# Layer B keys: softmax weights multiplied into the features instead of the values, token sums of 128 feature rows by 68 columns

## The chip, the cores and the metric

The kernel runs on one core of a Trainium2 chip. A core has five engines that run side by side and meet only at semaphores: TensorE (PE, the matrix unit, which writes to PSUM), VectorE (DVE), ScalarE (ACT), GpSimd (POOL) and SyncE (SP, which here issues the DMA transfers). The metric is the device time of one execution in microseconds (us); the figure for the kernel before is the median of three runs.

## What is computed

Two pairs of layers are applied to a token matrix of 2048 rows by 512 columns, A, B, A, B, each with a layer norm ahead of it and its result added to the rows. Layer A is attention inside four segments of 512 tokens plus a memory carried between segments. Layer B, which the change touches, is linear attention with softmax features, for 32 heads of 16 columns:

```
pq = einsum('bhsd,hdf->bhsf', q, w_phi)
pk = einsum('bhsd,hdf->bhsf', k, w_phi)
phi_q = concatenate([softmax(pq), softmax(-pq)], axis=-1)
phi_k = concatenate([softmax(pk), softmax(-pk)], axis=-1)
kv = einsum('bhsf,bhsd->bhfd', phi_k, v)
z = einsum('bhsf->bhf', phi_k)
o = einsum('bhqf,bhfd->bhqd', phi_q, kv) / (einsum('bhqf,bhf->bhq', phi_q, z)[..., None] + 1e-06)
```

A key thus has two softmaxes of 16 features for each head, one of each sign, and each has its own sum of exponentials. One divided by that sum is the key's softmax weight. The token sum kv needs feature times weight times value, and it does not matter to the sum which of the two factors carries the weight.

## The kernel before

A `Graph` collects operations with what each reads and writes, and tiles from fixed pools of buffers. Nothing is scheduled when the kernel is built: a compressed table, `ORDER`, holds for all operations their order, then one byte for each that names its engine, then one byte for each tile that names its buffer. `emit` walks that order, gives each engine its instructions in it, and adds the semaphore waits. An operation whose result may be made by ACT or DVE (`evac`, which copies PSUM to SBUF) has its engine from that table. So the order of every engine is fixed beforehand, and each engine works strictly through its own list.

PSUM is used as four buffers of 128x1024 (`D` in the profile). SBUF pools that matter here: `p2` (128x1024 bf16, in the profile `p`, like `p1`), `pT` (value tiles) and `pS` (small sums).

The stages in time are: layer A's four segments of the first pair, with layer B's keys of each segment (`b_keys`) as soon as its rows are done; then the four `b_query` of that pair, which need the token sums of all segments, mixed with layer A of the second pair and with its keys; last the four `b_query` of the second pair. All token sums of a pair must be complete before its first query is divided, so the keys of segments 2 and 3 (c = 2 and 3) stand just before that point.

`b_keys` takes the tokens in units of two tiles of 128 tokens (n = 2) or one (n = 1): per pair of layers seven units of two and two units of one, the latter in segment 3. For a unit of two it does this:

1. `BK` projects the keys with the folded weight, 16 matmuls of 512 columns on 64 rows (line 341, a helper that also records all other projections).
2. `kexp` on ACT (line 351, the helper of every ACT function): two exponentials of 128x1024, one of each sign, into two tiles.
3. `Zred` on DVE (line 1003): two sums over 16 features, giving 32 sums for each token and sign.
4. The weights, one over the sums: on DVE (`rZ`, line 393) for c = 0 and 1, on ACT as Ln and Exp (`zkl`, line 351) for c = 2 and 3. They are written into row 16 of the value tile `Vt` (pool `pT`).
5. `BV` projects the values; then `Vt` multiplies the values by the weights, once for each sign. For c = 0 to 2 one DVE operation for each token tile reads PSUM and writes 1024 columns (line 1039). For c = 3 the values are first copied to SBUF (`BVe`) and two DVE operations of 512 columns follow for each tile (line 1031).

When four tiles are through (three and one in segment 3), `KV` adds up the tokens: for each of eight slots (a group of eight heads and a sign) the 128 exponentials of the eight heads are the matmul's weights, and 136 columns of `Vt` (17 by 8 heads) move through. Each token tile takes 16 matmuls, two for each slot, because the 128 tokens are split into two halves of 64 rows that run side by side in the array. Over the two pairs these are 512 matmuls `D<-pT,p` of line 341, in two PSUM buffers for each of the ten parts. `kv_add` adds each PSUM buffer into `KV32` on DVE (line 969), and at the last part multiplies by a 0/1 mask, because only the blocks of equal heads are wanted: `Rkv` (line 973) and the column of sums `Rz1` (line 976). `Zq` in `b_query` (line 326) uses `Rz1`, `N` uses `Rkv`.

`setup` makes the constants and `fold_weights` the folded weights. There the value weight is permuted by four `evac` named `perm`, and `Wbd`, from which the folded weights come, is made from `w_phi` and the mask.

## Time and profile before

| | |
|---|---|
| median of three runs | 459.82 us (459.4 to 461.3) |
| the profiled execution | 464.63 us |
| its span in the profile | 462.9 us |
| POOL busy | 59.2 us (13% of the span) |
| the DMA engines' mean share, queue q1 | 41.3% |
| granted TensorE clock, mean | 0.998 |

The profile is of one execution. It gives each engine's busy time, groups of equal instructions (line of the kernel, engine, operation, what is written and read, how often; then total busy time, mean duration of one in ns, and the idle time before them), the instructions in order of time, and the chain of work that ended last, followed back from the last instruction. An instruction's duration holds a fixed part that overlaps with the next one, so the distance between two starts is what one costs in a row of equal ones. A name with `<-` reads "written from".

### The profile page before, as it was taken

The numbers are of one execution on the slowest core, as the hardware profiler recorded it, in microseconds if no ns is written. First come the engines' busy times: TensorE is split into PE (matmuls) and PEld (weight loads), VectorE is DVE, ScalarE is ACT, GpSimd is POOL, SyncE is SP. The second block draws the span as 40 slices with busy tenths as digits, with TensorE's granted clock in tenths as the row PEclk, the third lists the DMA queues.
The fourth block names the chain that finished last, engine by engine and source line by source line (L and its number), as shares of the span: only waits on it lengthen the run. The fifth ranks groups of instructions, "written<-read, shape, count | busy, mean of one in ns | idle before, by whom it ended". The sixth has DMA issues, their size and how long they took to land.

```text
span 462.9 us, 26150 instructions
## 1 busy us (share of the span) xinstructions
PE 431.9 (93%) x12085; PEld 293.1 (63%) x12085; DVE 409.3 (88%) x760; ACT 418.2 (90%) x559; POOL 59.2 (13%) x143
## 2 busy tenths in 40 slices
PE   8999879899999989998899998999999989899896
PEld 4666647567666666765455767666676567556553
DVE  6999978798799987887999999998898896899897
ACT  6999989899999998689999999999999899577992
POOL 2530023001101001100330212110011020110000
PEclk9999999999999999999999999999999999999999
DMA  8967664354334231100356575365332423400156
GB/s 260 207 135 126 107 112 83 59 120 65 66 73 98 28 50 27 36 3 6 45 106 111 81 98 97 73 110 78 46 50 37 111 49 42 47 13 3 38 83 195
DMA packets 105168, 36.71 MB, mean 79 GB/s; under 512 B 91731, under 2 KB 105059, under 8 KB 105059
## 3 DMA queue, kind: packets, MB, share of 16 engines
q1 hardware_dynamic: 104226, 34.50, 41.3%
q8 instruction: 95, 1.56, 1.4%
q10 hardware_dynamic: 800, 0.52, 0.4%
q14 instruction: 15, 0.11, 0.1%
q0 software_dynamic: 32, 0.02, 0.0%
HBM read 10.76 MB, written 6.55 MB: 37 GB/s over the span
## 4 chain that ended last, share of the span: by engine, by line
PE 58%; ACT 20%; DVE 12%; DMA 4%; issue 3%; POOL 1%; SPq 0%; DVEq 0%; ACTq 0%
PE D L341 38%; PE D L326 20%; ACT p L351 12%; ACT pP L351 6%; DVE stats L594 3%; DMA pX<-p 2%; DVE X L956 2%; DMA p<-p 2%; DVE p L615 1%; DVE pQ L681 1%; DVE p L1120 1%; ACT pS L351 1%; POOL rstd L604 1%; DMA X<-in_A_x_dram 1%; DVE p L360 1%
## 5 line engine op out<-in xcount | busy, mean ns | idle before, releaser
L351 ACT ACTIVATE p<-D 128x1024 bf16<-128x1024 f32 (+1 forms) x228 | 223.6, 1027 | 14.9 <-PE D L341 12.1
L351 ACT ACTIVATE pP<-D 128x640 bf16<-128x640 f32 (+2 forms) x192 | 149.7, 830 | 8.8 <-PE D L326 7.8
L326 PE MATMUL D<-pK,pQ 64*128 64x256 bf16 (+6 forms) x1792 | 111.4, 227 | 4.5 <-ACT pP L351 1.6
L326 PEld LDWEIGHTS D<-pK,pQ 64*128 64x128 bf16 x1792 | 65.3, 93 | 37.6 <-ACT pP L351 6.9
L326 PE MATMUL D<-pW,pP 64*128 64x50 bf16 (+1 forms) x3072 | 85.0, 181 | 0.8 <-ACT pP L351 0.4
L326 PEld LDWEIGHTS D<-pW,pP 64*128 64x128 bf16 x3072 | 68.8, 93 | 6.5 <-issue 1.3
L602 POOL TENSOR_SCALAR rstd<-mv 128x1 f32<-128x1 f32 x60 | 16.9, 285 | 347.2 <-DVE mv L595 346.9
L326 PE MATMUL D<-pW,p 64*128 64x50 bf16 (+1 forms) x2048 | 49.4, 181 | 0.9 <-issue 0.8
L326 PEld LDWEIGHTS D<-pW,p 64*128 64x128 bf16 x2048 | 43.6, 93 | 4.5 <-issue 1.2
L956 DVE TENSOR_TENSOR X<-X,D 128x1024 bf16<-128x1024 bf16 (+1 forms) x36 | 39.2, 1097 | 5.6 <-PE D L341 5.0
L594 DVE BATCH_NORM_STATS2 stats<-X 128x6 f32<-128x512 bf16 x63 | 42.1, 681 | 1.7 <-DMA X<-in_A_x_dram 1.6
L1003 DVE TENSOR_REDUCE pS<-p 128x64 f32<-128x1024 bf16 (+1 forms) x36 | 39.1, 1091 | 2.1 <-ACT p L351 1.9
L326 PE MATMUL D<-tri,rep 64*128 64x64 bf16 (+1 forms) x384 | 39.9, 197 | 0.5 <-issue 0.5
L341 PE MATMUL D<-pX,WA_q 64*128 64x512 bf16 (+1 forms) x288 | 37.1, 353 | 1.3 <-ACT p L351 1.3
L341 PE MATMUL D<-pX,WA_k 64*128 64x512 bf16 (+1 forms) x288 | 37.0, 353 | 0.2 <-ACT pP L351 0.2
L341 PE MATMUL D<-WB_k,pX 64*128 64x512 bf16 (+1 forms) x288 | 33.5, 353 | 3.9 <-DMA pX<-p 3.1
L604 POOL TENSOR_TENSOR rstd<-rstd,mhalf 128x1 f32<-128x1 f32 x60 | 35.9, 603 | 4.0
L341 PE MATMUL D<-WB_v,pX 64*128 64x512 bf16 (+1 forms) x288 | 34.4, 353 | 1.8 <-issue 1.8
L341 PE MATMUL D<-WA_o,p 64*128 64x512 bf16 (+1 forms) x288 | 33.1, 352 | 1.6 <-DMA p<-p 1.5
L341 PE MATMUL D<-WB_o,p 64*128 64x512 bf16 (+1 forms) x288 | 32.6, 353 | 1.8 <-ACT pP L351 0.8
L341 PE MATMUL D<-WA_v,pX 64*128 64x512 bf16 x256 | 33.0, 377 | 0.8 <-DVE p L360 0.8
L341 PE MATMUL D<-pX,WB_q 64*128 64x512 bf16 x256 | 32.8, 376 | 0.2
(123 smaller groups left out, 675.7 us busy)
## 6 DMA issues: line engine op xcount, KB each, us to landing
v_rows<-pV SPq DMA_DIRECT2D x16, 272.0 KB, 3.1
pW<-v_rows SPq DMA_DIRECT2D x64, 68.0 KB, 3.1
out_dram<-X SPq DMA_DIRECT2D x7, 256.0 KB, 2.7
X<-in_A_x_dram SPq DMA_DIRECT2D x3, 512.0 KB, 5.8
pX<-in_B_wqkv_dram SPq DMA_DIRECT2D x3, 512.0 KB, 5.0
p<-p SPq DMA_TRANSPOSE x73, 3.1
pX<-p SPq DMA_TRANSPOSE x54, 3.5
WA_k<-in_A_wk_dram SPq DMA_DIRECT2D x2, 256.0 KB, 5.3
```

The source lines that it names most:

```text
L326: ins = e.matmul(out_ap, lhsT, rhs, start=st, stop=sp, tile_position=(basep(lhsT), basep(out_ap)))
L341: ins = e.matmul(out_ap, lhsT[64 * hf:64 * hf + 64], rhs[64 * hf:64 * hf + 64], start=k == 0 and i == 0, stop=k == 1 and i == len(lists[hf ...
L351: return self.g.op({"act": (dur, lambda e: e.activation(out_ap(), in_ap(), func, scale=scale))}, reads, writes, opens, label=label)
L360: "dve": ((340 if fast else n / 0.96 + 65), lambda e: e.tensor_copy(out_ap(), in_ap()))}
L594: v(lambda e: e.bn_stats(self.stats[:, t, :], self.X[:, t, :]), 602, [R("X", t)], [R("st", t)], label="bn")
L602: v(lambda e: e.tensor_scalar(rs, self.mv[:, t, 1:2], LN_EPS, None, op0=ALU.add), 170, [R("mv", t)], [R("rstd", t)], eng="pool", label="rstd")
L604: v(lambda e: e.tensor_tensor(rs, rs, self.mhalf[:], ALU.pow), 540, [R("rstd", t), R("mhalf")], [R("rstd", t)], eng="pool", label="rstd")
L615: v(lambda e: e.tensor_scalar(xn.t[:], self.X[:, t, :], self.mv[:, t, 0:1], self.rstd[:, t:t + 1], op0=ALU.subtract, op1=ALU.mult), 300, [ ...
L681: ch = {"dve": (129 + n / 3.84, lambda e, sl=sl, out=out: e.tensor_scalar(out(), src(), self.m4[:, sl:sl + 1], None, op0=ALU.mult))}
L956: self.v(lambda e: e.tensor_tensor(X(), X(), src(), ALU.add), 65 + 512 * n / 0.96, pr + xr, xr, label="res")
L1003: fn = lambda e, sgn=sgn, eo=eo, Z=Z, n=n: e.tensor_reduce(Z.t[:, 0:64 * n].rearrange("p (k s h) -> p k s h", k=n, s=2)[:, :, sgn, :], eo( ...
L1120: v(lambda e, Ns=Ns, Tm=Tm, w=w, shape=shape: e.tensor_tensor(shape(Tm.t[:]), shape(Ns.t[:]), w(), ALU.mult), 600, [Ns, AB[0]], [Tm], labe ...
```

## The change

The weight goes into the exponentials. The value tile becomes a plain copy of the projected values, with a 17th row that is set to 1 once for each buffer in `setup`. The columns of the folded weights and of the value weight are permuted so that heads lie in fours; an exponential tile now belongs to one token tile and holds, for each group of four heads, both signs side by side (128 columns).

For a unit of two, `kexp` is four ACT operations of 512 columns instead of two of 1024. `Zred` is again two of 1024 columns, but the 16 features that it sums now lie four elements apart. The weights are written to a small tile; for c = 2 and 3 ACT makes them with one Ln and one Exp of 128 (before, one Ln of 128 and two Exp of 64). The new `kn` multiplies the exponentials in place on DVE, one operation of 1024 columns for each token tile. `BVe` copies the values out of PSUM in all units. `KV` has eight slots again, each a group of four heads with both signs, and 68 moving columns (17 by 4 heads), so that one PSUM buffer holds what two held. `kv_add` therefore runs once for each part, and the masked copies at its end are made in four pieces of 64 rows each, `Rkv` and `Rkz`, in which a piece may move from one half of the partitions to the other.

Pool `p2` grows from 19 to 21 buffers, `pT` shrinks from 5 to 4, and `ORDER` is a new table. What the engine bytes of the two tables say:

| operations | before | after |
|---|---|---|
| all on PE, ACT, DVE | 1185, 558, 760 | 1165, 583, 766 |
| `kexp` on ACT | 36 | 64 |
| `zkl` on ACT | 18 | 12 |
| `BVe` on ACT | 6 (2 of 1024 columns, 4 of 512) | 11 (7 and 4) |
| `BVe` on DVE | 0 | 7 (of 1024) |
| `Vt`, then `kn`, on DVE | 40 | 36 |
| `KVacc` on DVE, ACT | 19, 1 | 10, 0 |
| `Rkv` and `Rkz` on DVE | 8 | 16 |
| `perm` on ACT, DVE | 2, 2 | 0, 4 |
| `Vev` (layer A's values) on ACT, DVE | 5, 11 | 3, 13 |

Six more copies and a mask go from one of the two engines to the other: to ACT one `Kev`, one `Km`, one `ote` and two `xnTe`; to DVE one `folde` and one `Macc`. In the new order the four `kexp` of a unit alternate between the two token tiles, except for seven pairs of neighbours that read the same half of a PSUM buffer. At the end of segment 3 the order on DVE is the last `KVacc`, four `Rkz`, four `Rkv`.

```diff
-        self.KV32 = sb("KV32", [128, 8, 136], F32)
-        self.Rkv = sb("Rkv", [128, 8, 16, 8], BF16)
+        self.KV32 = sb("KV32", [128, 8, 68], F32)
+        self.Rkv = sb("Rkv", [128, 8, 16, 4], BF16)
+        self.h4 = sb("h4", [128, 4], F32)
...
-        self.pT = pool("pT", N_VT, [128, 2, NG, 17, 8], BF16, {}, ("Vt",))
+        self.pT = pool("pT", N_VT, [128, 2, 8, 17, 4], BF16, {}, ("Vt",))
...
-        v(lambda e: e.tensor_copy(self.Rz1[:, :, 1, :], self.H8[:, None, :].to_broadcast([128, 8, 8])), 130,
-          [R("H8")], [R("RzH")])
+        v(lambda e: e.tensor_reduce(self.h4[:], self.ident[:].rearrange("p (a h) -> p h a", h=4), AX.X, ALU.add), 250, [R("ident")], [R("h4")], label="one")
+        v(lambda e: e.tensor_copy(self.Rz1[:].rearrange("p i k (u h) -> p (i k u) h", h=4), self.h4[:, None, :].to_broadcast([128, 32, 4])), 210,
+          [R("h4")], [R("RzH")] + [R("Rz", q, h) for q in range(2) for h in range(2)], label="one")
+        for i, tp in enumerate(self.pT.tensors):
+            self.pT.init[i] = two(lambda e, tp=tp: e.memset(tp[:, :, :, 16, :], 1.0), 200.0, 130.0)
...
+            self.evac(lambda g=g: self.WB["v"][:, g, :].rearrange("p (a d h) -> p a d h", a=8, h=4),
+                      lambda g=g: self.WBraw["v"].t[:, g, :].rearrange("p (a h d) -> p a d h", a=8, h=4),
                       512, [self.WBraw["v"]], [R("WBv", g)], label="perm")
...
+        for u in range(2):
+            v(lambda e, u=u: e.tensor_tensor(Wbd.t[:].rearrange("p (g u j h) -> p u g h j", g=NG, u=2, h=4)[:, u],
+                                             self.wphi_st[:, :, None, :].to_broadcast([128, NG, 4, 16]),
+                                             self.H8[:, None, 4 * u:4 * u + 4, None].to_broadcast([128, NG, 4, 16]), ALU.mult), 340,
+              [R("wphi"), R("H8")], [Wbd[u]])
...
-    def kv_add(self, ps, q, first, last):
+    def kv_add(self, ps, first, last):
...
+        src = lambda: ps.t[:].rearrange("p (b x) -> p b x", b=2)[:, :, 0:272]
+        dst = lambda: self.KV32[:].rearrange("p (b k) c -> p b (k c)", b=2)
         if first:
-            self.evac(dst, src, 136 * n, [ps[0]], [R("KV32", q)], label="KVacc")
+            self.evac(dst, src, 544, [ps[0]], [R("KV32")], label="KVacc")
...
+            v(lambda e: e.tensor_tensor(dst(), dst(), src(), ALU.add), 65 + 544 / 0.96, [ps[0], R("KV32")], [R("KV32")], label="KVacc")
         if last:
...
+            for sgn in range(2):
+                for hf in range(2):
+                    ri, ro = slice(64 * sgn, 64 * sgn + 64), slice(64 * hf, 64 * hf + 64)
+                    kv = lambda ri=ri, hf=hf: self.KV32[ri].rearrange("p (g u) (c h) -> p g u c h", u=2, h=4)[:, :, hf]
+                    v(lambda e, kv=kv, ri=ri, ro=ro, sgn=sgn: e.tensor_tensor(self.Rkv[ro].rearrange("p (g s) c h -> p g s c h", s=2)[:, :, sgn], kv()[:, :, 0:16, :],
+                                                                              self.h4[ri, None, None, :].to_broadcast([64, NG, 16, 4]), ALU.mult),
+                      65 + 256 / 0.96, [R("KV32"), R("h4")], [R("Rkv", sgn, hf)], label="Rkv")
+                    v(lambda e, kv=kv, ri=ri, ro=ro, sgn=sgn, hf=hf: e.tensor_tensor(self.Rz1[ro].rearrange("p (g s) k h -> p g s k h", s=2)[:, :, sgn, 0, 4 * hf:4 * hf + 4],
+                                                                                     kv()[:, :, 16, :], self.h4[ri, None, :].to_broadcast([64, NG, 4]), ALU.mult),
+                      85, [R("KV32"), R("h4")], [R("Rz", sgn, hf)], label="Rkz")
...
     def b_keys(self, L, c, parts):
...
                 S = self.T(self.pD, "gen")
                 Z = self.T(self.pS, "Z")
                 Et = [self.T(self.p2, "ET") for _ in range(n)]
...
+                cols = lambda E: E.t[:].rearrange("p (g s f h) -> p g s f h", g=8, s=2, h=4)
+                zs = lambda k, Z=Z: Z.t[:, 64 * k:64 * k + 64].rearrange("p (g s h) -> p g s h", g=8, s=2)
+                ws = lambda k, Z=Z: Z.t[:].bitcast(BF16)[:, 256 + 64 * k:256 + 64 * k + 64].rearrange("p (g s h) -> p g s h", g=8, s=2)
                 for k, tt in enumerate(u):
+                    E = Es[tt] = Et[k]
+                    for sgn in range(2):
+                        self.act(lambda E=E, sgn=sgn: E.t[:].rearrange("p (a g s x) -> p a g s x", a=2, g=4, s=2)[:, :, :, sgn, :],
+                                 lambda S=S, u=u, k=k: self.tview(S, u, k).rearrange("p (a g x) -> p a g x" if len(u) == 2 else "p a (g x) -> p a g x", **({"a": 2} if len(u) == 2 else {}), g=4),
+                                 ACT.Exp, 512, [S[512 * k]], [E[sgn]], scale=1.0 - 2.0 * sgn, label="kexp")
+                        if n == 1:
+                            v(lambda e, E=E, sgn=sgn, k=k, zs=zs, cols=cols: e.tensor_reduce(zs(k)[:, :, sgn, :], cols(E)[:, :, sgn].rearrange("p g f h -> p g h f"), AX.X, ALU.add),
+                              65 + 512 / 0.96, [E[sgn]], [Z[(k, sgn)]], label="Zred")
+                    if n == 2:
+                        v(lambda e, E=E, k=k, Z=Z: e.tensor_reduce(Z.t[:, 64 * k:64 * k + 64], E.t[:].rearrange("p (a f h) -> p a h f", a=16, h=4), AX.X, ALU.add),
+                          65 + 1024 / 0.96, [E[0], E[1]], [Z[(k, 0)], Z[(k, 1)]], label="Zred")
+                allz = [Z[(k, sgn)] for k in range(n) for sgn in range(2)]
+                allw = [Z[("w", k, sgn)] for k in range(n) for sgn in range(2)]
+                if n == 2 and (L, c) not in ZKD:
+                    self.act(lambda Z=Z: Z.t[:, 0:128], lambda Z=Z: Z.t[:, 0:128], ACT.Ln, 128, allz, allz, psum=False, label="zkl")
+                    self.act(lambda Z=Z: Z.t[:].bitcast(BF16)[:, 256:384], lambda Z=Z: Z.t[:, 0:128], ACT.Exp, 128, allz, allw, scale=-1.0, psum=False, label="zkl")
+                for k, tt in enumerate(u):
+                    E = Es[tt]
+                    for sg in ((0,), (1,)) if n == 1 else ((0, 1),):
+                        a, b = sg[0], sg[-1] + 1
+                        if not (n == 2 and (L, c) not in ZKD):
+                            v(lambda e, k=k, a=a, b=b, zs=zs, ws=ws: self.recip(e, ws(k)[:, :, a:b, :], zs(k)[:, :, a:b, :]), self.dur_recip(32 * (b - a)),
+                              [Z[(k, x)] for x in sg], [Z[("w", k, x)] for x in sg], label="rZ")
+                        v(lambda e, E=E, k=k, a=a, b=b, cols=cols, ws=ws: e.tensor_tensor(
+                            cols(E)[:, :, a:b], cols(E)[:, :, a:b], ws(k)[:, :, a:b, None, :].to_broadcast([128, 8, b - a, 16, 4]), ALU.mult) if b - a == 1 else e.tensor_tensor(
+                            cols(E).rearrange("p g s f h -> p (g s) f h"), cols(E).rearrange("p g s f h -> p (g s) f h"),
+                            ws(k).rearrange("p g s h -> p (g s) h")[:, :, None, :].to_broadcast([128, 16, 16, 4]), ALU.mult),
+                          65 + 535 * (b - a) / 2, [Z[("w", k, x)] for x in sg] + [E[x] for x in sg], [E[x] for x in sg], label="kn", port=True)
                 ps = self.T(self.pD, "gen")
...
+                Vt = self.T(self.pT, "Vt")
+                for k, tt in enumerate(u):
+                    Vts[tt] = (Vt, k)
+                self.tproj(ps, lambda dt: self.WB["v"][:, dt, :], [R("WBv", g) for g in range(NG)], u, lhs, [xT[tt] for tt in u], opens=[Vt], label="BV")
+                self.evac(lambda Vt=Vt, n=n: Vt.t[:, 0:n].rearrange("p k (b g) c h -> p (k b) g (c h)", b=3 - n)[:, :, :, 0:64],
+                          lambda ps=ps, n=n: ps.t[:].rearrange("p (a x) -> p a x", a=2)[:, :, 0:256 * n].rearrange("p a (g x) -> p a g x", x=64), 512 * n, [ps[0], ps[512]][:n], [Vt], label="BVe")
+            ps = self.T(self.pD, "gen")
+            self.pair(lambda ps=ps, part=part, Es=Es, Vts=Vts: [
+                [(ps.t[:, b * 512 + k * 68:b * 512 + (k + 1) * 68], Es[tt].t[:, (4 * b + k) * 128:(4 * b + k + 1) * 128],
+                  Vts[tt][0].t[:, Vts[tt][1], 4 * b + k].rearrange("p c h -> p (c h)"))
+                 for k in range(4) for tt in part] for b in range(2)],
+                [68] * (4 * len(part)), [Es[tt][sgn] for tt in part for sgn in range(2)] + list(dict.fromkeys(Vts[tt][0] for tt in part)),
+                [ps[0]], label="KV")
+            self.kv_add(ps, c == 0 and part[0] == 0, c == 3 and part[-1] == 3)
...
-N_XT, N_KM, N_K1, N_K2, N_VT, N_SM, N_QT, N_V, N_VS = 5, 3, 10, 19, 5, 6, 3, 2, 3
+N_XT, N_KM, N_K1, N_K2, N_VT, N_SM, N_QT, N_V, N_VS = 5, 3, 10, 21, 4, 6, 3, 2, 3
...
-VCOP = {(0, 3), (1, 3)}
```

More of the change, by code (lines that the diff above doesn't have):

```diff
@@ L583, in fold_weights @@
                                                     Wbd.t[64 * hf:64 * hf + 64, g * 128 + hf * 64:g * 128 + hf * 64 + 64], True, True) for g in range(NG) for hf in range(2)],
-                        [], [W[dt], Wbd], [ps], label="fold", rows=64, dur=112.0)
+                        [], [W[dt], Wbd[0], Wbd[1]], [ps], label="fold", rows=64, dur=112.0)
                 self.evac(lambda k=k, dt=dt: self.WB[k][:, dt, :].rearrange("p (g h c) -> p h g c", g=NG, h=2),
@@ L1084, in b_query @@
             for sgn in range(2):
-                self.mm(lambda sgn=sgn, gp=gp: zq(gp, sgn), [], [EQ[(gp, sgn)], R("RzH")] + [R("Rz", q) for q in range(2)], [ZQ[(gp, sgn)]], label="Zq", rows=64, dur=204)
+                self.mm(lambda sgn=sgn, gp=gp: zq(gp, sgn), [], [EQ[(gp, sgn)], R("RzH")] + [R("Rz", q, x) for q in range(2) for x in range(2)], [ZQ[(gp, sgn)]], label="Zq", rows=64, dur=204)
         zr = [ZQ[(gp, sgn)] for gp in range(2) for sgn in range(2)]
```

187 lines of the change are left out of this document (57 added, 130 removed).

## The prediction

> **What bounds the kernel now.** The page's head comes first: how busy each engine is, and, from the chain that ended last, on which engine the end hangs.
>
> ```profile
> span 462.9 us, 26150 instructions
> ...
> PE 431.9 (93%) x12085; PEld 293.1 (63%) x12085; DVE 409.3 (88%) x760; ACT 418.2 (90%) x559; POOL 59.2 (13%) x143
> ...
> PE 58%; ACT 20%; DVE 12%; DMA 4%; issue 3%; POOL 1%; SPq 0%; DVEq 0%; ACTq 0%
> ```
>
> PE, ACT and DVE are each busy for 88 to 93% of the span; none alone is the bound. Shares are averages over stages, so I next read stretches of time, each row with the busy time of PE, PEld, DVE, ACT and POOL:
>
> ```profile
> 100.00:130.00 30.00, 29.31 (x938) 21.22 (x934) 25.64 (x46) 29.18 (x38) 3.27 (x8) 1.00 0.42 71
> 130.00:160.00 30.00, 29.67 (x918) 20.26 (x916) 28.15 (x46) 29.50 (x39) 2.43 (x6) 1.00 0.37 75
> 185.00:206.00 21.00, 20.93 (x348) 14.77 (x346) 19.18 (x38) 16.04 (x23) 1.58 (x4) 1.00 0.09 21
> 206.00:240.00 34.00, 30.51 (x816) 18.24 (x814) 29.78 (x65) 32.64 (x50) 6.86 (x12) 1.00 0.25 46
> 400.00:428.00 28.00, 26.88 (x404) 16.43 (x406) 25.04 (x46) 20.27 (x28) 2.23 (x5) 1.00 0.10 17
> ```
>
> In the attention stretches (100 to 160) PE and ACT are both 97 to 99% busy: extra work on either costs time, and less work on PE alone may win nothing. The two stretches in which a pair's last keys are summed (185 to 206, 400 to 428) differ: PE 20.93 of 21 and 26.88 of 28, ACT only 16.04 and 20.27, DVE 19.18 and 25.04. The chain in order of time (start, us, what) says the same:
>
> ```profile
> 185.71 7.19 PE D L341 x128
> 193.01 12.43 PE D L341 x192
> ...
> 402.37 12.58 PE D L341 x144
> 415.06 12.13 PE D L341 x224
> ```
>
> From 185.71 to 205.5 and from 402.37 to 427.2 the end hangs on PE without a break, on line 341's projections and token sums. Right behind, from 206 to 240, ACT is busy for 32.64 of 34.
>
> **The change part by part.** *Token sums on PE.* Lines in order of time (start, us, and what). A matmul's own duration holds a part that overlaps with the next, so the distance between starts is what it costs in a row.
>
> ```profile
> 414.90 1.58 PE L341 MATMUL D<-pT,p 64*128 64x136 bf16 x48
> 416.32 1.91 PE L341 MATMUL D<-WB_k,pX 64*128 64x256 bf16 x32
> ...
> 429.15 0.40 PE L326 MATMUL D<-Rkv,p 64*128 64x64 bf16 x16
> 429.40 0.78 PE L326 MATMUL D<-Rz,p 64*128 64x48 bf16 x49
> ```
>
> 48 matmuls of 136 columns take 416.32 - 414.90 = 1.42 us, 29.6 ns each. Their number stays 512, each with its load of 128 columns, but 68 columns move. The nearest row is `b_query`'s N: 64 rows, 128 loaded columns for each matmul, 64 moving; 16 take 429.40 - 429.15 = 0.25 us, 15.6 ns each. Bounds: 29.6 (the load sets the distance) and 15.6. I take 15.6, from which it differs by four columns. PE is relieved of 512 x 14.0 ns = 7.2 us. In the order of time 128 of the 512 stand in 185.71 to 205.5 and 128 in 400 to 428, where PE alone is the bound: 256 x 14.0 = 3.6 us off the path. The other 256 lie in attention, beside an equally full ACT; of their 3.6 us I count half, 1.8, between 0 and 3.6.
>
> A rule of the Trainium skill speaks against this: "TensorE: Matmul & The Clock Gate", section "Back-to-back issue gap", says that in a stream of load and matmul pairs both set the distance, about 81 ns at 128 columns. By it fewer columns would gain little, and the PE term would be near 0 instead of 5.4. The 15.6 ns of N, with a load for each matmul, does not agree.
>
> *DVE.* Groups (busy us, mean ns of one):
>
> ```profile
> L1003 DVE TENSOR_REDUCE pS<-p 128x64 f32<-128x1024 bf16 x28 | 33.8, 1210 | 1.8 <-ACT p L351 1.7
> L1039 DVE TENSOR_TENSOR pT<-D,pT 128x1024 bf16<-128x1024 f32 x24 | 28.3, 1215 | 2.6 <-PE D L341 2.3
> ...
> L1120 DVE TENSOR_TENSOR p<-p,pS 128x1024 bf16<-128x1024 bf16 x32 | 21.6, 683 | 1.0 <-ACT p L351 0.9
> ...
> L360 DVE CAST pV<-D 128x1024 bf16<-128x1024 f32 x11 | 13.4, 1222 | 1.9 <-PE D L341 1.7
> ...
> L969 DVE TENSOR_TENSOR KV<-KV,D 128x544 f32<-128x544 f32 x16 | 11.0, 716 | 3.6 <-PE D L341 3.6
> ...
> L1031 DVE TENSOR_TENSOR pT<-p,pT 128x512 bf16<-128x512 bf16 x16 | 6.2, 411 | 0.3 <-ACT p L359 0.3
> ...
> L1003 DVE TENSOR_REDUCE pS<-p 128x32 f32<-128x512 bf16 x8 | 5.3, 672 | 0.3 <-ACT p L351 0.2
> ...
> L360 DVE COPY WB_v<-pX 128x512 bf16<-128x512 bf16 x2 | 1.3, 629 | 0.0
> ```
>
> Gone: `Vt`, 24 x 1215 + 16 x 411 ns = 35.7 us, and nine `KVacc`, 9 x 716 = 6.4. New: `kn`, with exactly the access of `nmul` in line 1120 (16 x 16 x 4, a weight for each four columns, both operands in SBUF): 28 x 683 + 8 x 411 ns = 22.4. Its other bound is the 1215 of a product from PSUM, at which it would cost 15 us more; the equal access decides for 683. New too: seven `BVe` at 1222, 8.6; the masked copies in four pieces, between 0 and another 3.2 (rows below), 1.4; two `Vev` and two `perm` taken over, 2.4 + 1.3; setup 0.7; the small moves (of the table in the section on the change, each between 0.3 and 1.2) together -1.4. Sum -6.7 us. `Zred` keeps its price although it now reads with a stride: its two shapes differ by 538 ns for 512 elements, 1.05 each, and `perm` (COPY WB_v), with a larger stride, took 629 for 512, under the 672 of a contiguous `Zred`. The other bound is the second rival. Of the 6.7 us I count 0 on the path: DVE has idle time in every stretch above but waits there for PE and ACT. At most it is the chain's 12% of it, 0.8.
>
> *ACT.* Four groups, then lines in order of time:
>
> ```profile
> L351 ACT ACTIVATE pS<-pS 128x128 f32<-128x128 f32 x28 | 9.0, 320 | 2.7 <-DVE pS L1003 2.6
> ...
> L359 ACT ACTIVATE pV<-D 128x1024 bf16<-128x1024 f32 x5 | 5.1, 1024 | 0.0
> ...
> L351 ACT ACTIVATE pT<-pS 128x64 bf16<-128x64 f32 x12 | 2.6, 249 | 0.2
> L359 ACT ACTIVATE WB_v<-pX 128x512 bf16<-128x512 bf16 x2 | 2.3, 1139 | 0.0
> ...
> 402.29 2.08 ACT L351 ACTIVATE p<-D 128x1024 bf16<-128x1024 f32 x2 [4.90 <-PE D L341]
> ...
> 417.84 2.06 ACT L351 ACTIVATE p<-D 128x512 bf16<-128x512 f32 x4 [0.40 <-PE D L341]
> ...
> 195.22 1.23 ACT L351 ACTIVATE p<-D 128x512 bf16<-128x512 f32 x2 [0.29 <-PE D L341]
> ```
>
> Five more `BVe` of 1024 at 1024 ns: 5.1 us. `zkl`: 12 x 249 ns go, 6 x 320 come: -1.1. `perm` and `Vev` that leave: 2 x 1.14 + 2 x 1.02 = 4.3. Small moves: five operations come and three go, +1.6. `kexp`: two of 1024 on one PSUM buffer take 2.08 (the second waits for the first), four of 512 that alternate 2.06, and two neighbours on one half 1.23, 0.14 more than alternating ones. So the fixed part of the two added instructions is hidden by the overlap that the order allows. Over 14 units with seven pairs of neighbours that is -0.3 + 1.0 = +0.7; with all as neighbours, 14 x 0.38 = 5.3. Sum +2.0 us. The key stretches hide it, where ACT is idle for 5 and 7.7 us; in attention it shows. I take half, 1.0, between 0 and 2.0, with 4.6 more if the splitting were not hidden.
>
> The Trainium skill, "ScalarE: Activation LUTs", section "What ACT_TABLE_LOAD costs", gives 186 ns and 0.833 ns for each column, less 93 ns of overlap between neighbours. By it a unit would take 2.17 us after and 1.99 before, 2.6 us more for 14 units. The trace agrees for four of 512 (2.06), but not for the two of 1024, which do not overlap here.
>
> *The end of a key stretch*, on DVE and PE:
>
> ```profile
> 426.30 1.35 DVE L969 TENSOR_TENSOR KV<-KV,D 128x544 f32<-128x544 f32 x2 [0.35 <-PE D L341]
> 427.57 0.31 DVE L976 TENSOR_TENSOR Rz<-KV,H 128x32 bf16<-128x32 f32 x2
> 427.80 1.29 DVE L973 TENSOR_TENSOR Rkv<-KV,H 128x512 bf16<-128x512 f32 x2
> ...
> 427.94 1.36 PE L326 MATMUL D<-Rz,p 64*128 64x48 bf16 x96 [0.77 <-DVE Rz L976]
> ```
>
> Behind the last `KV` of a pair stand two `KVacc` (1.35 us), `Rz`, then `Zq` on PE. Now there is one `KVacc`, 0.7: -0.64. Four `Rkz` replace two that took 0.31: between 0.31 and 0.76; two start 0.12 apart, so 0.55: +0.24. For both pairs -0.8 us. The `Rkv` behind are covered by 96 `Zq` matmuls (1.2 us); uncovered they cost 0.4.
>
> *Buffers and setup.* No row prices the buffer changes (one `pT` fewer, two `p2` more, ten PSUM uses fewer): 0, between one eviction's 1.2 us lost and won. Setup and the moved copies have loads and layer A beside them: 0, at most 0.7.
>
> **The sum.** -3.6 - 1.8 + 1.0 - 0.8 = -5.2 us. The profiled execution took 464.63 us (span 462.9, 1.7 around it): 459.4. The runs' median, 459.82, is 0.98965 of it: 454.7.
>
> **The rivals.** *ACT paces it.* For it: ACT is 97 to 98% busy in attention and at 32.64 of 34 behind the first key stretch, and it gets 2.0 us more. Then attention wins nothing, and half of what the key stretches win is waited for behind them: -1.8 - 0.8 + 2.0 = -0.6, 464.0, or 459.2. Against it: the chain lies on PE for 58%, on ACT for 20%.
>
> *The strided sum becomes the bound* (the slower side). At two cycles for each element, `Zred`'s 28 x 1024 + 8 x 512 = 32768 elements cost 34.4 us more: DVE 409.3 - 6.7 + 34.4 = 437.0, above PE's 431.9 - 7.2 = 424.7. With PE's present idle time (31.0) the span is 468.0, the execution 469.7, the median 464.9. DVE overtakes PE from 22.1 us on, 0.67 ns more for each element. Against it: `perm`'s 629 ns.
>
> *All of PE's saving counts*, with DVE's 0.8, and ACT's work is hidden: -7.2 - 0.8 - 0.8 = -8.8, 455.8, or 451.1. For it: the chain's 58%. Against it: the full ACT.
>
> *The matmuls don't get shorter*, since the load of 128 columns sets 29.6 ns: -0.8 + 1.0 = +0.2, 464.8, or 460.0. Against it: 15.6 ns. The skill's rule above would have it so.
>
> **How the numbers follow.** Forecast 0.52, ACT 0.20, strided sum 0.08, all of PE 0.12, no shorter matmuls 0.04; 0.04 for waits of the new order that no row of the old one shows, on the slower side. Under 0.5% (2.3 us) a measurement of this kernel can hardly tell a difference from none (its runs: 459.4 to 461.3). Faster 0.52 + 0.12 = 0.64; same 0.20 + 0.04 = 0.24; slower 0.12. The forecast's own bounds, -8.0 to -2.4 us, give 451.9 to 457.4. The range reaches to all cases but the slower: 451.0 to 461.0.
>
> **What would show it.** `D<-pT,p` with 68 columns about 16 ns apart; PE busy for about 425; `Zred` near 1210, `kn` near 683; a unit's four `kexp` in about 2.1 us; both key stretches about 2 us shorter, PE still unbroken; one `KVacc` before the `Rkz`. Wrong it would be if `Zred` or `kn` took the upper bound, or if ACT stayed at 98% in attention while PE's idle time grew there by what its matmuls save.

## The result, and the profile after

| | before | after |
|---|---|---|
| median of 16 runs each, side by side | 462.52 us (459.4 to 465.0) | 456.18 us (453.48 to 459.84) |
| the profiled execution | 464.63 us | 456.51 us |
| its span | 462.9 us | 454.8 us |

The ratio is 0.9868, with a 95% interval of 0.984 to 0.9896: the change makes the kernel 1.3% faster, some 6 us. (A ratio, here and below, is formed from runs in the faster of the two states in which executions come, and is not exactly the quotient of the medians given.) The forecast was 454.7 us against the 459.82 known then, a ratio of 0.9889. The number was close; the experiments below show that the way to it was not right.

First the head of the page of the kernel after:

```profile
span 454.8 us, 26184 instructions
...
PE 427.2 (94%) x12085; PEld 289.5 (64%) x12085; DVE 403.1 (89%) x766; ACT 420.9 (93%) x584; POOL 58.4 (13%) x146
...
PE 61%; ACT 20%; DVE 12%; issue 3%; DMA 3%; POOL 1%; DVEq 0%
```

Against the head of before, PE has 4.7 us less, DVE 6.2 us less and ACT 2.7 us more. The span of this profile fell by 8.1 us, more than any one engine's work did. The groups of the changed operations (busy us, mean ns of one):

```profile
L351 ACT ACTIVATE p<-D 128x512 bf16<-128x512 f32 x64 | 35.1, 615 | 2.8 <-PE D L341 2.2
L1015 DVE TENSOR_REDUCE pS<-p 128x64 f32<-128x1024 bf16 x28 | 33.4, 1211 | 0.9 <-ACT p L351 0.9
L1030 DVE TENSOR_TENSOR p<-p,pS 128x1024 bf16<-128x1024 bf16 x28 | 18.5, 678 | 1.0 <-ACT pS L351 0.8
L341 PE MATMUL D<-pT,p 64*128 64x68 bf16 x512 | 11.0, 191 | 0.6 <-issue 0.3 <-ACT pP L351 0.2
L360 DVE CAST pT<-D 128x1024 bf16<-128x1024 f32 x7 | 8.5, 1220 | 0.3 <-PE D L341 0.3
L359 ACT ACTIVATE pT<-D 128x1024 bf16<-128x1024 f32 x7 | 7.2, 1022 | 0.0
L983 DVE TENSOR_TENSOR Rz<-KV,h 64x16 bf16<-64x16 f32 x8 | 1.4, 170 | 0.1
```

The main prices of the prediction hold: the strided `Zred` takes 1211 ns (1210 before), `kn` 678 (683 was taken), `BVe` 1220 and 1022 (1222 and 1024). The open question is what these savings did to the end. For that I mark three places in the order of time that both kernels have: the 32 products with `WA_o` at the start of the first key stretch, the first product with `Rz` behind that stretch, and the same behind the second. First the timeline of PE in the kernel before (start, us, what):

```profile
186.49 1.92 PE L341 MATMUL D<-WA_o,p 64*128 64x256 bf16 x32
...
192.25 0.65 PE L341 MATMUL D<-pT,p 64*128 64x136 bf16 x16
192.72 0.30 PE L380 MATMUL D<-ident,p 64*128 64x64 bf16 x8
...
203.79 0.77 PE L341 MATMUL D<-pT,p 64*128 64x136 bf16 x16
...
206.36 0.95 PE L326 MATMUL D<-Rz,p 64*128 64x48 bf16 x64
```

and that of the kernel after:

```profile
181.41 1.91 PE L341 MATMUL D<-WA_o,p 64*128 64x256 bf16 x32
...
185.99 0.66 PE L341 MATMUL D<-pT,p 64*128 64x68 bf16 x32
186.48 1.03 PE L341 MATMUL D<-WB_v,pX 64*128 64x512 bf16 x8
...
200.21 1.16 PE L326 MATMUL D<-Rz,p 64*128 64x48 bf16 x80 [0.23 <-DVE Rz L983]
...
419.21 1.16 PE L326 MATMUL D<-Rz,p 64*128 64x48 bf16 x80 [0.75 <-DVE Rz L983]
```

32 token-sum products now take 186.48 - 185.99 = 0.49 us, 15.3 ns each (15.6 was forecast). The second stretch of before ends at 427.94 (quoted in the prediction). A second profile of the same kernel, of the next batch (span 457.3), has the three marks at

```profile
183.19 1.91 PE L341 MATMUL D<-WA_o,p 64*128 64x256 bf16 x32
...
201.99 1.16 PE L326 MATMUL D<-Rz,p 64*128 64x48 bf16 x80 [0.23 <-DVE Rz L983]
...
421.74 1.16 PE L326 MATMUL D<-Rz,p 64*128 64x48 bf16 x80 [0.75 <-DVE Rz L983]
```

Against before this gives, with the forecast's terms set out by place beside it (its 0.8 us of attention split in two halves):

| us gained | profile after | second profile after | forecast |
|---|---|---|---|
| up to the first key stretch | 5.1 | 3.3 | 0.4 |
| in the first key stretch | 1.1 | 1.1 | 2.2 |
| from there to the end of the second | 2.6 | 1.8 | 2.6 |
| behind it | -0.6 | -0.6 | 0 |

So about half of the gain or more arose ahead of the first key stretch, with the first pair's attention, where the forecast had next to nothing, and the first key stretch gave half of what it should. A single profile is rough in the first row: in the four profiles of the old order (before and e8 to e10 below) the first mark stands between 184.7 and 188.4 us, in the five of the new order (both of after, e1, e3, e7) between 181.4 and 185.5, in the mean 3.6 us apart. The kernel after, run again with the experiments:

> The changed kernel itself, on the same chip as the three experiments beside it, so that each can be set against it. All theories: the ratio to the kernel before stays near 0.987 (about -6 us).

458.27 us (457.19 to 462.39) against 465.51 in the same batch, ratio 0.9857 (0.9815 to 0.99): the same gain. A part of it goes with the granted clock. All six runs of the kernel after show 0.999 or more. Of the 21 of the kernel before, nine show 0.998 or more (median 463.65 us) and twelve 0.994 to 0.996 (465.75 us). Against the nine the gain is 5.4 us in place of 7.2; no run shows whether the change itself brings the higher clock. One batch differs from another by a few us in both kernels, so below only ratios, or times of one batch, are compared.

### The profile page after: what moved, and what is told of

The parts are those of the page before. It is cut to its first block, busy times and chain, and to the rows that moved or that the text cites. A ratio compares the mean times of both kernels' runs of the same rounds, so it can differ in the third digit from the quotient of the medians.

```text
span 454.8 us, 26184 instructions
## 1 busy us (share of the span) xinstructions
PE 427.2 (94%) x12085; PEld 289.5 (64%) x12085; DVE 403.1 (89%) x766; ACT 420.9 (93%) x584; POOL 58.4 (13%) x146
## 4 chain that ended last, share of the span: by engine, by line
PE 61%; ACT 20%; DVE 12%; issue 3%; DMA 3%; POOL 1%; DVEq 0%
PE D L341 38%; PE D L326 22%; ACT p L351 11%; ACT pP L351 7%; DVE X L961 2%; DVE pQ L686 1%; DVE p L1117 1%; DVE stats L599 1%; DMA pX<-p 1%; DMA p<-p 1%; ACT pS L351 1%; DVE p L620 1%; DMA X<-in_A_x_dram 1%; DVE pK L360 1%; DVE p L906 1%
## 5 line engine op out<-in xcount | busy, mean ns | idle before, releaser
L326 PE MATMUL D<-pK,pQ 64*128 64x128 bf16 (+6 forms) x1792 | 112.0, 227 | 4.2 <-ACT p L351 1.0
L326 PEld LDWEIGHTS D<-pK,pQ 64*128 64x128 bf16 x1792 | 67.0, 93 | 40.2 <-ACT pP L351 8.5
L326 PE MATMUL D<-pW,pP 64*128 64x50 bf16 (+1 forms) x3072 | 84.0, 181 | 3.4 <-issue 2.7
L326 PE MATMUL D<-pW,p 64*128 64x50 bf16 (+1 forms) x2048 | 50.4, 181 | 0.4 <-DVE pQ L686 0.2
L1015 DVE TENSOR_REDUCE pS<-p 128x64 f32<-128x1024 bf16 x28 | 33.4, 1211 | 0.9 <-ACT p L351 0.9
L341 PE MATMUL D<-WB_v,pX 64*128 64x512 bf16 (+1 forms) x288 | 33.3, 352 | 0.0
```

The costliest lines, as they stand in the source:

```text
L326: ins = e.matmul(out_ap, lhsT, rhs, start=st, stop=sp, tile_position=(basep(lhsT), basep(out_ap)))
L341: ins = e.matmul(out_ap, lhsT[64 * hf:64 * hf + 64], rhs[64 * hf:64 * hf + 64], start=k == 0 and i == 0, stop=k == 1 and i == len(lists[hf ...
L1015: v(lambda e, E=E, k=k, Z=Z: e.tensor_reduce(Z.t[:, 64 * k:64 * k + 64], E.t[:].rearrange("p (a f h) -> p a h f", a=16, h=4), AX.X, ALU.ad ...
```

## The experiments

### Giving work back to the kernel after

The first three put work of one engine back and touch neither order nor buffers.

**TensorE.** Three of the four groups of token sums move 136 columns again (the 68 twice, the second copy unread):

```diff
+ twice = lambda o, k: bass.AP(o.tensor, o.offset, [o.ap[0], [272, 2 if k < 3 else 1], [1, 68]])
- out: ps[..68 columns]           moving: Vt[..68 columns]
+ out: twice(ps[..68 columns], k) moving: Vt[..][:, None, :].to_broadcast([128, 2 if k < 3 else 1, 68])
```

> The changed kernel, order and engines untouched, but three of the four groups' token-sum matmuls move 136 columns again: the 68 columns twice, the second time into PSUM columns that nobody reads. That gives PE back 384 x 14.0 ns = 5.4 us of work and nothing to anyone else. Theory of the prediction (all of PE's saving counts in the key stretches, half of it in attention): 192 of these 384 lie in the key stretches, so 2.7 + 1.35 = 4.0 us slower than the changed kernel, ratio to before about 0.996. Rival 'ACT paces': at most 1.4 us, about 0.990. Rival 'order and buffers made the gain': under 1 us, about 0.988. Rival 'all of PE's saving counts': 5.4 us, about 0.9985.

461.6 us, ratio 0.9922 (0.9892 to 0.9951): 3.3 us slower than the kernel after in the same batch, for 5.4 us of matmuls, between the 1.4 of "ACT paces" and the 4.0 of the prediction's theory. In its timeline of PE the first key stretch reads:

```profile
183.47 1.91 PE L341 MATMUL D<-WA_o,p 64*128 64x256 bf16 x32
...
203.33 1.16 PE L326 MATMUL D<-Rz,p 64*128 64x48 bf16 x80
```

19.86 us against 18.80 after. 96 of the 128 products in it are wide again, 96 x 14.0 ns = 1.3 us, of which 1.06 show. In this order PE's time in the key stretch counts for the most part.

**ScalarE.** All 18 evictions of the values go to ACT (its busy time rises from 420.9 to 427.1), and DVE loses seven, 8.5 us:

```diff
- BVe: 11 on ACT, 7 on DVE
+ BVe: 18 on ACT
```

> The changed kernel with all 18 value copies on ACT: the seven of DVE go over, at the same places of the order. ACT gets 7 x 0.92 = 6.4 us (distance of starts), DVE loses 8.5. Theory of the prediction (ACT's work counts half, DVE's not at all): 3.2 us slower than the changed kernel, ratio about 0.994. Rival 'ACT paces': 6.4 us, about 1.001. Rival 'PE alone is the bound': no change, 0.987; were DVE the bound, faster.

464.3 us, ratio 0.9973 (0.9942 to 1.0003): 6.0 us slower than the kernel after, for 6.2 to 6.4 us of ScalarE work, although DVE was relieved of 8.5 us at the same time. Eight of its 12 runs show a clock of 0.996 or less and none of the kernel after does; the four at 0.999 or more have a median of 463.0 us, 4.7 us above the kernel after. So more than the prediction's half counts, 4.7 to 6.0 us, and the rival's price of 6.4 is nearer than the 3.2; the intervals are too wide to say how near. Both key stretches keep their length (18.80 and 21.47 us, after 18.80 and 21.46), so it is paid outside them.

**VectorE.** Six of the 28 strided sums are done twice, the first time into unread columns:

```diff
- e.tensor_reduce(Z.t[:, 64 * k:64 * k + 64], ...)
+ [e.tensor_reduce(Z.t[:, z:z + 64], ...) for z in ((192, 64) if k == 1 and u[0] == 0 and c > 0 else (64 * k,))][-1]
```

> The kernel after with 6 of its 28 strided sums of the keys' features done twice, once into columns that nobody reads: 6 x 1.211 = 7.3 us of VectorE work put back, a little more than the 6.2 us by which its busy time fell; order, buffers, TensorE and ScalarE as in the kernel after. Theory of the prediction (VectorE's saving lies beside other work and counts at 0 to 0.8 us): at most 1 us slower than the kernel after, ratio to the kernel before 0.985 to 0.990. Rival (VectorE's saving is what the terms of TensorE and ScalarE leave open, about 3 us): 2.5 to 4 us slower than the kernel after, ratio 0.992 to 0.997. Were all of it on the path: 7 us, 1.00.

461.06 us, ratio 0.9943 (0.9907 to 0.998). The group shows the six more:

```profile
L1015 DVE TENSOR_REDUCE pS<-p 128x64 f32<-128x1024 bf16 x34 | 40.2, 1211 | 0.7 <-ACT p L351 0.5
```

0.9943 - 0.9868 = 0.0075 of 464.2 us: 3.5 us slower than the kernel after, about half of 7.3. The intervals of the two ratios do not overlap. The first key stretch, which holds one doubled sum of 1.21 us, is longer by 1.13 in the profile (183.00 to 202.93); PE waits 1.14 us in it for an addition of the token sums (line 973). In this order DVE's time there isn't covered either.

If giving back told what taking away is worth, the sum would now be whole: 0.62 x 7.2 of PE, half of DVE's 6.2, less some 1.9 for ACT's 2.0, about 5.7 us. The next runs show that it does not.

### Taking work out of the kernel before

Order, engines and buffers are those of the kernel before; only the size of single instructions changes.

**TensorE alone.**

```diff
- ps.t[:, b * 512 + k * 136:b * 512 + (k + 1) * 136],      Vts[tt].t[...]
+ ps.t[:, b * 512 + k * 136 + 68:b * 512 + (k + 1) * 136], Vts[tt].t[...][:, 68:136]
```

> The kernel before, its order, engines and buffers untouched; each token-sum product moves the last 68 of its 136 columns alone (the other 68 columns of the sums are left out, what stands in the buffer is added in their place). So TensorE alone has 7.2 us less work (512 x 14.0 ns), ScalarE and VectorE have what they had. The term of the prediction (a half to all of it counts, by the stretch): -5.4 us, ratio 0.988. By e1_wide (62% of what was given back): -4.4 us, 0.9905. Rival, ScalarE paces the stretches: -1.8 us or less, 0.996 or above. Rival, all of it counts: -7.2 us, 0.9845.

466.13 us against 465.58, ratio 1.0004 (0.9971 to 1.0038). 512 products are as short as in the kernel after, and nothing is won that shows: by the interval at most 0.3%, 1.4 us, of 7.2. Its timeline of PE in the first key stretch shows where a good part of it went:

```profile
188.38 1.92 PE L341 MATMUL D<-WA_o,p 64*128 64x256 bf16 x32
...
193.45 0.42 PE L341 MATMUL D<-pT,p 64*128 64x68 bf16 x16
194.55 0.29 PE L380 MATMUL D<-ident,p 64*128 64x64 bf16 x8 [0.68 <-DVE p L615]
...
205.55 0.68 PE L341 MATMUL D<-pT,p 64*128 64x68 bf16 x16 [0.38 <-DVE KV L969]
...
208.16 0.95 PE L326 MATMUL D<-Rz,p 64*128 64x48 bf16 x64
```

The stretch takes 208.16 - 188.38 = 19.78 us, before 206.36 - 186.49 = 19.87. Of PE's 128 x 14 ns = 1.8 us, 1.06 turned into waits for DVE that the timeline lists: 0.68 at the transposes, 0.38 at the last token sum. In the kernel before these two rows (quoted above, 192.72 and 203.79) show no wait, so the chain named PE. But the timeline of DVE in the kernel before shows hardly any room either; its idle time stands in brackets:

```profile
191.24 0.42 DVE L615 TENSOR_SCALAR p<-X,mv,rstd 128x512 bf16<-128x512 bf16 x1 [0.20 <-POOL rstd L604]
...
193.05 0.42 DVE L360 COPY pX<-D 128x512 bf16<-128x512 bf16 x1 [0.41 <-PE D L380]
...
200.62 0.76 DVE L1031 TENSOR_TENSOR pT<-p,pT 128x512 bf16<-128x512 bf16 x2 [0.26 <-ACT p L359]
...
204.49 1.35 DVE L969 TENSOR_TENSOR KV<-KV,D 128x544 f32<-128x544 f32 x2 [0.19 <-PE D L341]
```

From 189.3 to 207.4 these are the only gaps that the timeline lists, 1.06 us in 18. So in this order the stretch had two engines without room, PE and DVE. In attention it was ACT that stayed full (windows of e8, PE, PEld, DVE, ACT, POOL):

```profile
100.00:130.00 30.00, 28.74 (x935) 20.40 (x928) 25.51 (x45) 29.20 (x37) 3.28 (x8) 1.00 0.39 78
130.00:160.00 30.00, 29.66 (x942) 20.53 (x940) 28.03 (x46) 29.50 (x38) 1.65 (x4) 1.00 0.40 76
```

PE is busy for 0.6 us less in the two than before, and ACT for 58.70 us of 60, as before (58.68).

**VectorE alone.**

```diff
- e.tensor_tensor(dst(), dst(), src(), ALU.add)
+ e.tensor_tensor(dst()[:, :, :, 100:136], dst()[:, :, :, 100:136], src()[:, :, :, 100:136], ALU.add)
```

> The kernel before, order, engines and buffers untouched; its 16 additions of the token sums add 36 of every 136 columns (the others keep their first values, left out), so that each goes from 0.716 us to about 0.30 us and VectorE alone has 6 to 7 us less work. The term of the prediction: 0 to -0.8 us, ratio 0.998 to 1.00. By e7_dve_back (some half of the 7.3 us given back showed): -3 us or more, 0.991 to 0.994; that would be the term that the prediction left out.

466.1 us, ratio 1.0 (0.9969 to 1.0031). Each addition takes 0.300 us in place of 0.716 (16 x 0.416 = 6.7 us), DVE is busy for 404.4 in place of 409.3, and nothing is won within 0.3%: as the prediction's term had it, and against the 3 us that e7 suggested.

**All three loads.**

```diff
+ the edits of e8 and e9
- e.activation(eo()[:, 0:2], S[:, 0:2], ACT.Exp, scale=...)
+ [e.activation(eo()[:, x:y], S[:, x:y], ACT.Exp, scale=...) for x, y in (((0, 1), (1, 2)) if n == 2 and sgn else ((0, 2),))][-1]
```

> The kernel before, order, engines and buffers untouched, with the three engines' loads of the change: the products of e8, the additions of e9, and 14 exponentials of the keys issued as two halves (ScalarE +14 x about 0.16 = 2 us). Nothing else of the change. If the work is all that the change brings (its order and buffers nothing): the sum -4.4 (TensorE) -3 (VectorE) +1.9 (ScalarE) = -5.5 us, ratio 0.988, the same as the kernel after. If the new order and buffers bring about half: -3 us, 0.9935. The prediction's own sum: -5.4 + 0 + 1.0 = -4.4 us, 0.9905.

463.84 us, ratio 0.9977 (0.995 to 1.0003): -0.2%, with an interval that just holds no change (the medians differ by 1.7 us). The page shows PE 428.1 and DVE 402.9 busy, the kernel after's 427.2 and 403.1; ACT stayed at 418.3 (418.2 before) in spite of its 14 more instructions, so that the run was if anything better off than meant. With the change's loads of PE and DVE, the old order and the old buffers win some 1 to 2 us of the 6 (0 to 2.3 by the interval). In the first key stretch PE still waits, for a row of the layer norm on DVE and for ACT:

```profile
190.77 0.29 PE L380 MATMUL D<-ident,p 64*128 64x64 bf16 x8 [0.59 <-DVE p L615]
...
201.91 0.54 PE L341 MATMUL D<-pT,p 64*128 64x68 bf16 x12 [0.32 <-ACT p L351]
```

The same two rows of each timeline give the length of the key stretches (first `WA_o` product to first `Rz` product):

| | first, us | second, us |
|---|---|---|
| before | 19.87 | 24.87 |
| e8, PE less | 19.78 | 24.55 |
| e9, DVE less | 19.87 | 24.04 |
| e10, both less | 19.58 | 23.74 |
| after | 18.80 | 21.46 |
| e1, PE back | 19.86 | 22.80 |
| e7, DVE back | 19.93 | 21.92 |
| e3, ACT more, DVE less | 18.80 | 21.47 |

The second stretch holds other work between the marks in the two orders, so its upper four rows compare only with each other, and so do the lower four. Less on one engine: 0 to 0.8 us. Less on both: 0.3 and 1.1, where the two apart add up to 0.1 and 1.2. More on either engine, in the other order: 0.5 to 1.3.

### Order and buffers

**The work of the change in the old order.** The kernel after, with each operation at the place and on the engine that its counterpart has before:

```diff
- order table of the change
+ the old table's sequence; kn where Vt stood, Rkz where Rz stood; buffers dealt anew
```

> The changed operations in the old order: every operation that both kernels have keeps the place and the engine of the old table, each new one stands where its forerunner stood (kn where Vt stood, one KV where the first of two stood, the halves of kexp where their whole stood, BVe just ahead of kn where there was none), and the buffers are dealt out anew. Theory of the prediction (the work makes the gain): the sum of -5.2 us holds up to a us or two, ratio 0.988 to 0.993. Rival 'order and buffers made the gain': near 1.000 or above.

481.45 us, ratio 1.0323 (1.0278 to 1.0368). Another order calls for another dealing of buffers, here by a simple rule (the free one left longest ago). So two controls keep each kernel's own order and deal its buffers by that rule:

```diff
  order, engines: as they are
- buffer of each tile: as in the table
+ buffer of each tile: of the free ones the one left longest ago
```

> The kernel after with its order and engines as they are; only the numbers of the buffers that the tiles get are dealt out anew (of the free buffers of a pool, the one left longest ago; 1185 of 1479 tiles get another). It is the control for e2_old_order, whose buffers were dealt in this way. Theory (the buffers' numbers don't matter, e2 lost its 21 us by its order): within 1 us of the kernel after, 455 to 459 us, 0.983 to 0.990 of the kernel before. Rival (the dealing cost e2 a good part): 462 us or more, ratio 0.997 or above.

> The kernel before with its order and engines as they are and its tiles' buffers dealt out anew by the same rule (1139 of 1509 tiles get another). It is the control for e6_order_alone. Theory: within 1 us of the kernel before, ratio 0.998 to 1.002. Rival (the dealing matters): 1.005 or more.

490.31 us, ratio 1.0551 (1.0509 to 1.0593), and 485.94 us, ratio 1.0454 (1.0411 to 1.0498). Both theories missed widely: the numbers of the buffers alone are worth 22 us in the kernel before and 32 after, three and a half and five times the change. Beside e5, e2 is 1.3% better with the same rule; beside e4, the new order is 2.2% worse than the old one. An accident of the dealing is thus larger than what was to be measured, and e2 settles nothing on the order.

**The old work in the new order**, dealt in the same way:

```diff
- order table of before
+ the change's sequence and engines for the work of before; buffers dealt anew
```

> The kernel before, with all its work (136-column token sums, values times weights, 8 two-column products at the end, 19 and 5 buffers) put in the order and on the engines of the kernel after, where an operation has a counterpart there; an operation that finds no free buffer comes as soon as there is one. Buffers dealt as in e5. Theory (the new order is worth about as much as the work's own terms leave open, some 3 us of the 6.1): ratio 0.990 to 0.996, 3 us or so below e5. Rival 1 (the work is all of it, the order nothing): 1.00, within 1 us of e5. Rival 2 (an order only fits the work for which it was found): slower, 1.005 or more; then this run says nothing on what the order is worth to the work after.

543.67 us, ratio 1.1698 (1.1651 to 1.1746): the second rival, an order that doesn't fit the work. It says nothing on what the order is worth to the work for which it was made.

**Which buffers.** Only the four PSUM buffers are dealt anew in the kernel after:

```diff
- buffer of each PSUM tile: as in the table
+ buffer of each PSUM tile: of the free ones the one left longest ago
```

> The kernel after with the PSUM buffers alone dealt out anew (508 of the 603 tiles of the pool of four get another), the SBUF buffers as in the kernel after. e4_slots_after, with all pools dealt anew, was 32 us slower. Theory (four PSUM buffers carry everything between the engines, and the number decides which evacuation a matmul waits for): most of it, 478 to 492 us, ratio 1.03 to 1.06. Rival (it is the SBUF buffers, 30 and more per pool group): within 5 us of the kernel after, below 1.00.

487.64 us, ratio 1.0486 (1.0455 to 1.0518), nearly all of e4's 1.0551. The group of attention's score products, first in the kernel after, then in this run (the column behind the second bar is PE's idle time ahead of them):

```profile
L326 PE MATMUL D<-pK,pQ 64*128 64x128 bf16 (+6 forms) x1792 | 112.0, 227 | 4.2 <-ACT p L351 1.0 <-ACT pP L351 0.6 <-DVE pV L360 0.3
```

```profile
L326 PE MATMUL D<-pK,pQ 64*128 64x128 bf16 (+6 forms) x1792 | 111.2, 227 | 17.4 <-ACT pP L351 2.5 <-DVE pV L360 2.4 <-DVE p L360 2.2
```

The same 1792 matmuls cost the same, but PE is idle for 17.4 us ahead of them in place of 4.2, and what the row names, for 7.1 of the 17.4, are readers of earlier PSUM tiles: a score product uses neither `pV` nor those `p`, it waits for their eviction out of the buffer it is to write. ACT in turn waits for PE (the view of the waits, after and then this run: us, times, longest):

```profile
ACT pP L351 <- PE D L326: 5.9, 15, 0.9
```

```profile
ACT pP L351 <- PE D L326: 20.0, 40, 1.6
```

A tile's buffer number decides whose reading its first matmul waits for; with four buffers and three full engines a wrong one is a wait of half a us on ACT (20.0 us in 40 waits).

## Why the prediction was right in its number and not in its way

*What held.* The spacing of the products (15.3 ns for 15.6), the prices on DVE and ACT, and that the strided sum costs nothing extra: the rival on the slower side falls with 1211 ns. The matmuls do get shorter, so the rival that has the load set the distance falls too. The rule of the Trainium skill beside it ("TensorE: Matmul & The Clock Gate", section "Back-to-back issue gap": load and matmul both set the spacing, about 81 ns for each matmul at N = 128) does not agree with this trace, 29.6 ns at 136 moving columns and 15.3 at 68, for products of 64 rows of which two run side by side.

*The step that failed* is the reading of the key stretches, "where PE alone is the bound". The chain there ran on PE without a break, and PE was busy for 20.93 of 21 us; I took DVE's 19.18 of 21 for room. It was none: between 189.3 and 207.4 DVE's gaps were four short waits, for PE (0.41 and 0.19), POOL (0.20) and ACT (0.26). e8 takes PE's 1.8 us out of that stretch and gets 0.09. The chain named one engine where a second would have ended within a few tenths of it. From the chain alone PE's term should have stood with 0 as its lower end in the key stretches too, as it did in attention.

*The PE term in attention* (1.8, between 0 and 3.6) did not show in the old order: e8's ACT stayed at 98% there, as the rival "ACT paces it" had it. The prediction's own sign of being wrong shows in the kernel after as well: from 100 to 160 us its ACT is busy for 58.79 of 60 (before 58.68), its PE for 57.70 (before 58.98). *The ACT term* (half of 2.0) was mis-sized: e3 shows 4.7 to 6.0 us for 6.2 to 6.4, so the +2.7 us of busy time cost nearer 2 to 2.5 than 1.0, as far as adding tells. The 0.7 above the 2.0 forecast lies in the exponentials: an estimate from the groups, (35.1 - 4.5) / 14 = 2.19 us for a unit of two (the 4.5 are the eight single ones of before), where the sum had 2.13. *The DVE term* (0) was right for DVE alone in the whole run (e9), though the second key stretch got 0.83 us shorter by it. That DVE kept PE's saving from showing is only part of it: with both relieved (e10) the first stretch gains 0.29 of the 2.2 forecast.

*The end of a key stretch* (-0.8) did not come. In the kernel after, the two last additions still stand side by side and the four `Rkz` take 0.72, not 0.55 (timeline of DVE):

```profile
197.93 1.48 DVE L973 TENSOR_TENSOR KV<-KV,D 128x544 f32<-128x544 f32 x2 [1.30 <-PE D L341]
199.44 0.72 DVE L983 TENSOR_TENSOR Rz<-KV,h 64x16 bf16<-64x16 f32 x4
```

From the start of the last products with `WB_q` to the first with `Rz` it is 2.37 us on PE (197.84 to 200.21), before 1.96 (204.40 to 206.36): 0.4 more where the forecast had 0.4 less.

*Order and buffers* (0 on the path) belong to the largest part. The loads without them are worth 0.2% (e10, 0 to 0.5% by its interval), the change 1.3%: some 4 to 6 of the 6 us come with what e10 lacks, together: the new order, the dealing of buffers, and the new dependencies (the values leave PSUM without waiting for the weights, and each part's token sum takes one PSUM buffer in place of two). The place of a large part of it shows in the stretches from 40 to 100 us, ahead of the first key stretch (PE, PEld, DVE, ACT, POOL; the kernel before, then e10, then the kernel after):

```profile
40.00:75.00 35.00, 30.73 (x932) 21.04 (x928) 30.75 (x59) 32.69 (x42) 3.89 (x9) 1.00 0.60 100
75.00:100.00 25.00, 22.87 (x686) 15.55 (x683) 21.15 (x36) 23.00 (x28) 3.12 (x8) 1.00 0.42 82
```

```profile
40.00:75.00 35.00, 29.84 (x912) 20.34 (x910) 29.98 (x58) 32.09 (x41) 3.28 (x8) 1.00 0.58 101
75.00:100.00 25.00, 24.68 (x744) 17.12 (x738) 22.86 (x39) 24.67 (x33) 3.74 (x9) 1.00 0.48 85
```

```profile
40.00:75.00 35.00, 33.23 (x994) 22.69 (x990) 32.98 (x68) 34.29 (x45) 5.15 (x14) 1.00 0.54 99
75.00:100.00 25.00, 24.96 (x820) 17.64 (x812) 24.10 (x40) 24.76 (x34) 1.18 (x3) 1.00 0.67 109
```

In these 60 us PE is idle for 6.4, 5.5 and 1.8 us, ACT for 4.3, 3.2 and 0.95. All four profiles of the old order have PE busy for 53.6 to 54.6 us there and ACT for 54.9 to 56.8; all five of the new order have 56.9 to 58.2 and 57.6 to 59.1. So here the new kernel fills gaps of all engines that the work taken out of the old one does not fill. The new order alone does not do it either: with its PSUM buffers dealt anew (e11) PE is busy for 51.9 us there. What opened these gaps is less plain. The chain of the kernel before holds three waits for transposing DMAs between 50 and 90 us (start, us):

```profile
50.91 2.58 DMA p<-p
...
62.36 4.37 DMA p<-p
...
81.76 4.45 DMA pX<-p
```

e9, in the same order, has all three again (from 51.65, 64.07 and 83.87), e8 and e10 the first two; the kernel after has one there (66.28, 4.52 us), its second profile, e1 and e3 none, e7 one. That sets the orders apart, but inside one order the number of these waits does not go with the first mark: e8, with two, has it at 188.38 us, before, with three, at 186.49; e3, with none, at 185.54, the kernel after, with one, at 181.41. It was not tested by itself: a run with one DMA moved earlier in the old order would have to deal buffers anew. How the 4 to 6 us split between dependencies, order and dealing stays open.

So the forecast's -5.2 us was met by other terms than its own, and that the number came close is luck. Of the 6.2 us that it counted for PE and for the end of the stretches, the old order pays out next to nothing, and the largest gain lies in what it set to 0.

## What to carry to other kernels

Where several engines are near 90% or more, what an edit gives back to one of them isn't what its removal gains: here 3.3 of 5.4 us of PE and 3.5 of 7.3 us of DVE show when added to one order, and nothing beyond the 0.3% of the interval when 7.2 or 6.7 are taken out of another. Before counting a saving on the engine that the chain names, look in the same stretch for the gaps of the next engine, one by one, with their releasers; if they are only a few tenths, the saving won't show by itself, and here relieving both engines in the old order won 1 to 2 us of 6. And when an order is changed for an experiment, a control with the same dealing of buffers comes first, since the PSUM buffers' numbers alone moved this kernel by 6%.

## What the runs showed of the hardware

Row-tiled products of 64 rows with a load of 128 columns each followed each other at a distance that goes with their moving columns: 15.3 ns for 68, 29.6 for 136, 0.22 to 0.23 ns for each column, so that the load set no floor here. A strided reduction on DVE (bf16, one element in four) costs what the contiguous one did, 1211 and 1210 ns for 1024. Two exponentials of 512 on one PSUM buffer, issued without a wait between them, cost ACT hardly more than one of 1024; the groups of e10 show it (line 1001 has the exponentials of the keys):

```profile
L1001 ACT ACTIVATE p<-D 128x512 bf16<-128x512 f32 x36 | 19.8, 610 | 1.4 <-PE D L341 1.1
...
L1001 ACT ACTIVATE p<-D 128x1024 bf16<-128x1024 f32 x14 | 14.4, 1027 | 6.7 <-PE D L341 6.6
```

Eight of the 36 are single and took 4.5 us in the kernel before, so the 14 pairs take (19.8 - 4.5) / 14 = 1.09 us each, one of 1024 takes 1.03; with a wait between the two it was 1.23 (quoted in the prediction). And the same program with the same order has profiles whose spans differ by 2.5 us (454.8 and 457.3), so that a single pair of spans can't carry a term under about 3 us, though the length of the first key stretch is 18.80 us in both.
